# The norm of one MLP chunk split in two, its factors ahead of the head-row moves on GpSimd, its turn ahead of a denominators' broadcast

## The chip, the cores and the metric

One core of a Trainium2 chip. The metric is the device time of one execution in microseconds (us). The kernel before takes 203.77 us (median of 6 executions, 203.6 to 209.71). Each execution is fast or slow; a slow one is over 1.5% above the fastest of its kernel.

Each kernel was executed five or six times beside the kernel before, and **one** execution left the trace that the profile shows. For the kernel before it is one more execution (204.51 us), which is not among the six.

## The reference, cut to what matters

```python
xn = layernorm(x)                        # x: 2048 x 512, bf16
s  = attention(xn) @ wo                  # 32 heads of 16, window of 8, dilation 2
h  = gelu(layernorm(xn) @ w1)            # then parts of h shifted by rows
x1 = xn + shifted(h) @ w2
g  = silu(x1 + gelu(layernorm(x1) @ w3) @ w4)     # w3: 512 x 1376
return x + s * g
```

The kernel works on rows of even and odd position ("parity" 0 and 1) and on four chunks of 512 rows. While TensorE does the attention of parity 0, unit by unit ("turns" 0 to 7), it also makes x1 of the chunks. Each x1 chunk is normalised on VectorE, stored to DRAM, and loaded back transposed ("turned"), because w3's matmuls need it with the features on the partitions. After the last unit come w3's matmuls, chunk after chunk.

## The kernel before: the parts that matter

```python
def layer_stats(src, name, lo, hi):      # VectorE: bn_stats, bn_aggr for each 128-row tile
    ...
    rsqrt_eps(rstd, mv[:, :, 1])         # two small GpSimd instructions: "the factors"

def ln3_norm(c, a=0, b=TPC):             # VectorE: (x - mean) * rstd for tiles a..b
    ...
    if b < TPC:
        return
    ln3_store(c)                         # SyncE: 512 KB to x1n_dram (L514)

def ln3_turn(c):                         # SyncE: transposing load into x1nT[c] (L519)
    nc.sync.dma_start_transpose(out=x1nT[c], in_=x1n_dram[c * CH : (c + 1) * CH, :])

def spread(p, lo, hi, q, ws, es):        # head-row moves: 8 DMAs for one w (L261)
    ...
def normalise_dn(p, r):   ...            # SyncE: reload denominators (L678)
def normalise_mid(p, r):  ...            # VectorE reciprocal (L697), SyncE store (L698)
def normalise_rr(p, r):   ...            # SyncE: broadcast load, 368 KB for (0, 0) (L707)
def normalise_end(p, r):  ...            # VectorE multiply (L714)

# late[n]: what is issued at the end of attention turn n
late[6] += [lambda: ln3_norm(1), lambda: normalise_dn(0, 1), lambda: ln3_turn(1)]
...
for n, p, r in ((3, 0, 0), (6, 0, 1), (N1 + 3, 1, 0), (N1 + 6, 1, 1)):
    ...
    if (p, r) != (0, 1):
        late[n + 2].append(lambda p=p, r=r: normalise_mid(p, r))
        late[n + 2].append(lambda p=p, r=r: normalise_rr(p, r))
for w in range(2):
    late[3 + 2 * w].append(lambda w=w: spread(1, 0, CUT, nc.gpsimd, (w,)))
```

SyncE issues its DMAs in program order, and one that waits holds up those behind it: in the trace of before it issued nothing from 79.99 to 83.28 us, while a broadcast waited. "Landing" below is the moment when a DMA's completion shows in the trace; "granted clock" is the share of TensorE's full clock that the throttle granted.

The softmax here doesn't subtract the row's maximum and nothing guards it: scores larger than these inputs give would overflow.

Of the kernel before, what the change touches and what calls it, by code (L numbers as in the profile page):

```python
# [15 lines left out]
def kernel(  # L16
# [14 lines left out]
    nc = tc.nc  # L31
# [52 lines left out]
    def at(kb, n, m):  # L84
        ar, o = (arenas[0], int(kb * KB)) if kb < 170 else (arenas[1], int((kb - 176) * KB))
        return ar[:, o : o + int(n * m)].rearrange("p (n m) -> p n m", n=n)
# [44 lines left out]
    for c in range(NCH):  # L131
        p, k = c // 2, c % 2
# [123 lines left out]
    def spread(p, lo, hi, q=nc.sync, ws=(0, 1), es=(0, 1)):  # L256
        for w in ws:
            for e in es:
                for gr in range(4):
                    r = 32 * gr + DH * e  # L260
                    q.dma_start(  # L261
                        out=(kT, qT)[w][e][r : r + DH, :, lo:hi], in_=kq[p][w][r : r + DH, :, lo:hi]
                    )
# [236 lines left out]
    def ln3_norm(c, a=0, b=TPC):  # L500
        p, k = c // 2, c % 2
        x_c = xn[p][:, k * TPC : (k + 1) * TPC, :]
        for lo, hi, mv, rstd in l3[c]:
            for j in range(max(lo, a), min(hi, b)):
                nc.vector.tensor_scalar(
                    out=xn3[:, j, :], in0=x_c[:, j, :], scalar1=mv[:, j - lo, 0:1],
                    scalar2=rstd[:, j - lo : j - lo + 1], op0=ALU.subtract, op1=ALU.mult,
                )
        if b < TPC:
            return  # L510
        ln3_store(c)

    def ln3_store(c):
        nc.sync.dma_start(  # L514
            out=x1n_dram[c * CH : (c + 1) * CH, :].rearrange("(i q) d -> q i d", q=P), in_=xn3
        )

    def ln3_turn(c):
        nc.sync.dma_start_transpose(out=x1nT[c], in_=x1n_dram[c * CH : (c + 1) * CH, :])  # L519
# [155 lines left out]
    def normalise_dn(p, r):  # L675
        n = H * runs[p][r][3] // P
        dn = small.tile([P, n], BF16, name="dn", tag="dn")
        nc.sync.dma_start(out=dn, in_=rrs[p, r][0].rearrange("h (a m) -> (h a) m", a=P // 8))  # L678
        rrs[p, r][0] = dn

    def pack(p, r):
        _, _, ra, rw = runs[p][r]
        for jj in range(2):
            for cg in range(4):
                hh = 4 * jj + cg
                nc.gpsimd.dma_start(  # L686
                    out=oT[p][DH * hh : DH * (hh + 1), :, ra : ra + rw],
                    in_=orw[p, r][32 * cg : 32 * cg + DH, jj],
                )

    def normalise_mid(p, r):
        _, _, ra, rw = runs[p][r]
        n = H * rw // P
        dn, rden_d = rrs[p, r]
        rb = small.tile([P, n], BF16, name="rb", tag="rb")
        with nc.allow_low_precision("bf16 weights"):
            nc.vector.reciprocal(out=rb, in_=dn)  # L697
        nc.sync.dma_start(out=rden_d.rearrange("h (a m) -> (h a) m", a=P // 8), in_=rb)  # L698

    def normalise_rr(p, r):  # L700
        _, _, ra, rw = runs[p][r]
        dn, rden_d = rrs[p, r]
        if p == 0 and r:
            rr = orws[r % 2][:, 0 : ND * rw]
        else:
            rr = at(rr_at[r % 2] if p else B0 + 8, 1, ND * rw)[:, 0, :]
        nc.sync.dma_start(out=rr, in_=rden_d.unsqueeze(1).to_broadcast([8, DH, ND * rw]))  # L707
        rrs[p, r] = rr
# [157 lines left out]
    late = {n: [] for n in range(len(order) + 4)}  # L866

    def st3(n, *ts):
        for t in ts:
            late[n].append(lambda t=t: ln3_stats(t // 4, t % 4, t % 4 + 1))  # L870
# [4 lines left out]
    st3(3, 4)  # L875
    st3(4, 5, 6)
    st3(5, 7)
    late[6] += [lambda: ln3_norm(1), lambda: normalise_dn(0, 1), lambda: ln3_turn(1)]

    w4s = [w4_tile(t) for t in range(S // P)]  # L880
    fill = {0: (0, 1), 1: (2,), 3: (3,), 4: (4,), 5: (5,), 7: (6,), 8: (7,)}
# [22 lines left out]
    for n, p, r in ((3, 0, 0), (6, 0, 1), (N1 + 3, 1, 0), (N1 + 6, 1, 1)):  # L904
        if (p, r) != (0, 1):
            late[n].append(lambda p=p, r=r: pack(p, r))
        if p:
            late[n].append(lambda p=p, r=r: normalise_dn(p, r))
        if (p, r) != (0, 1):
            late[n + 2].append(lambda p=p, r=r: normalise_mid(p, r))  # L910
            late[n + 2].append(lambda p=p, r=r: normalise_rr(p, r))
    late[N1 + 7].append(lambda: normalise_end(1, 0))
    CUT = 480
    for w in range(2):
        late[3 + 2 * w].append(lambda w=w: spread(1, 0, CUT, nc.gpsimd, (w,)))

    prev = None

# [73 lines left out]
    for t in range(8, 15):  # L992
# [5 lines left out]
        p, i = fq.pop(0)  # L998
# [50 lines left out]
```

## Time and profile before

| | before |
|---|---|
| median, six executions | 203.77 us |
| profiled execution | 204.51 us (span of the trace 202.7) |
| TensorE busy | 193.9 us, 96% of the span |
| wait of TensorE for chunk 1's turned rows | 0.75 us |

The span runs from the first to the last instruction; the measured time is about 1.8 us longer. The two ordinary fast executions that I had when I predicted took 203.62 and 203.76. (Of the six in the table four took 203.6 to 203.8, one 204.65, and one, 209.71, is slow.)

### The profile page before, as it was taken

How to read it: one execution, taken by the hardware profiler on the slowest of the kernel's cores; microseconds unless marked ns; L12 is line 12 of the kernel's file. 1: busy time of each engine (PE TensorE's matmuls, PEld its weight loads, DVE VectorE, ACT ScalarE, POOL GpSimd, SP SyncE). 2: the span in 40 equal slices, each digit the busy share in tenths (PEclk: the TensorE clock that was granted, in tenths of full speed). 3: DMA queues.
4: the chain of work that ended last, by engine and by line, in shares of the span. 5: the costliest groups of instructions: out<-in, count | busy, mean ns of one | idle time of the engine just before them, and what ended most of it. 6: DMA issues, size and time to landing. Idle time of an engine off the chain costs nothing.

```text
span 202.7 us, 4886 instructions
## 1 busy us (share of the span) xinstructions
PE 193.9 (96%) x1939; PEld 95.2 (47%) x1967; DVE 134.2 (66%) x263; ACT 131.5 (65%) x155; POOL 73.8 (36%) x146
## 2 busy tenths in 40 slices
PE   7899999999999999999899999999999999999991
PEld 2585445444444444444444444444455444444460
DVE  5788889735298988888610501188567968676683
ACT  2367665859988888885555575998788879212120
POOL 4899516200033195978750000003830590700000
PEclk9999999999999999999999999999999999999998
DMA  5993266367750189487979846793130052554221
GB/s 133 359 349 96 83 145 120 62 102 115 151 205 5 52 178 137 80 236 157 185 220 198 258 102 102 156 333 126 32 55 5 8 126 35 115 168 155 86 78 53
DMA packets 33734, 27.17 MB, mean 134 GB/s; under 512 B 14720, under 2 KB 31624, under 8 KB 33712
## 3 DMA queue, kind: packets, MB, share of 16 engines
q1 hardware_dynamic: 31520, 23.64, 46.7%
q0 software_dynamic: 2048, 3.09, 8.4%
q8 instruction: 15, 0.25, 0.5%
q10 hardware_dynamic: 144, 0.13, 0.2%
q14 instruction: 7, 0.06, 0.1%
HBM read 12.82 MB, written 4.98 MB: 88 GB/s over the span
## 4 chain that ended last, share of the span: by engine, by line
PE 83%; DMA 7%; DVE 3%; POOL 3%; issue 2%; DVEq 0%; POOLq 0%
PE w_ps L567 18%; PE w_ps L530 13%; PE qk_ps L432 8%; PE v_ps L596 7%; PE w_ps L488 7%; PE w_ps L465 7%; PE wo_ps L742 6%; PE s_ps L621 6%; PE o_ps L644 4%; PE qk_ps L450 4%; DMA x1n_dram<-arena 3%; DMA arena<-x1n_dram 3%; PE w_ps L547 1%; DMA arena<-in_A_x_dram 1%; DVE l0s L311 1%
## 5 line engine op out<-in xcount | busy, mean ns | idle before, releaser
L626 ACT ACTIVATE arena<-s_ps 128x960 bf16<-128x960 f32 (+1 forms) x68 | 62.8, 976 | 12.3 <-PE s_ps L621 12.3
L567 PE MATMUL w_ps<-arena 128*128 128x512 bf16 (+1 forms) x164 | 39.3, 368 | 0.5 <-issue 0.2
L534 ACT ACTIVATE arena<-w_ps 128x1024 bf16<-128x1024 f32 x20 | 20.5, 1025 | 14.2 <-PE w_ps L530 14.2
L686 POOL DMA_DIRECT2D arena<-orw x48 | 24.9, 526 | 5.8 <-DVE orw L656 5.8
L567 PEld LDWEIGHTS <-arena 128*128 128x128 bf16 x187 | 17.6, 98 | 18.9
L530 PEld LDWEIGHTS <-arena 128*128 128x128 bf16 x160 | 15.4, 98 | 20.2 <-DMA arena<-x1n_dram 1.2
L752 POOL TENSOR_TENSOR arena<-arena 128x512 bf16<-128x512 bf16 x6 | 7.7, 1302 | 47.1 <-DVE arena L751 47.1
L432 PE MATMUL qk_ps<-arena 128*128 128x512 bf16 (+1 forms) x109 | 20.2, 332 | 0.6 <-ACT arena L328 0.5
L656 DVE CAST orw<-o_ps 128x960 bf16<-128x960 f32 (+1 forms) x17 | 19.7, 1157 | 1.5 <-PE o_ps L644 1.4
L573 DVE TENSOR_TENSOR arena<-w_ps,arena 128x512 bf16<-128x512 f32 (+1 forms) x17 | 11.2, 659 | 14.2 <-PE w_ps L567 14.1
L601 DVE CAST v_aug<-v_ps 128x512 bf16<-128x512 f32 x17 | 11.7, 690 | 10.3 <-PE v_ps L596 10.2
L582 ACT ACTIVATE arena<-arena 128x512 bf16<-128x512 bf16 (+1 forms) x9 | 5.3, 584 | 20.4 <-DVE arena L573 20.4
L530 PE MATMUL w_ps<-arena,arena 128*128 128x512 bf16 x78 | 17.3, 379 | 0.9 <-DMA arena<-x1n_dram 0.7
L530 PE MATMUL w_ps<-arena 128*128 128x512 bf16 x78 | 17.7, 379 | 0.2
L596 PE MATMUL v_ps<-wv_sb,arena 128*128 128x512 bf16 x68 | 17.5, 380 | 0.0
L621 PEld LDWEIGHTS <-arena 32*128 32x128 bf16 x544 | 10.2, 92 | 14.5 <-issue 14.4
L621 PE MATMUL s_ps<-arena 32*128 32x120 bf16 (+1 forms) x544 | 15.9, 213 | 0.0
L488 PE MATMUL w_ps<-arena 128*128 128x512 bf16 x64 | 15.3, 380 | 0.0
L492 DVE TENSOR_TENSOR arena<-w_ps,arena 128x512 bf16<-128x512 f32 x16 | 10.4, 684 | 7.2 <-PE w_ps L488 7.2
L439 ACT CAST arena<-qk_ps 128x1024 bf16<-128x1024 f32 x11 | 11.1, 1021 | 6.0 <-PE qk_ps L432 6.0
L432 PEld LDWEIGHTS <-arena 128*128 128x128 bf16 x112 | 10.8, 98 | 8.3 <-issue 0.5
L280 POOL TENSOR_SCALAR l3r<-l3m 128x1 f32<-128x1 f32 (+2 forms) x11 | 2.6, 236 | 33.2 <-DVE l3m L289 33.1
(108 smaller groups left out, 275.9 us busy)
## 6 DMA issues: line engine op xcount, KB each, us to landing
x1n_dram<-arena SPq DMA_DIRECT2D x5, 512.0 KB, 4.0
arena<-in_A_x_dram SPq DMA_DIRECT2D x4, 512.0 KB, 6.0
arena<-in_A_x_dram SPq DMA_DIRECT2D x6, 256.0 KB, 6.8
out_dram<-arena SPq DMA_DIRECT2D x6, 256.0 KB, 2.1
arena<-in_B_w_dram SPq DMA_DIRECT2D x1, 1376.0 KB, 7.0
arena<-in_B_w_dram SPq DMA_DIRECT2D x1, 1280.0 KB
arena<-arena SPq DMA_DIRECT2D x16, 72.0 KB, 2.5
arena<-arena SPq DMA_DIRECT2D x16, 68.0 KB, 2.6
```

What stands on the lines that cost most here:

```text
L432: nc.tensor.matmul(pt[:, b, hh * w : (hh + 1) * w], lhsT=wqk_sb[:, dt, nt * P : (nt + 1) * P], rhs=xnT[p][:, dt, k * CH + hh * w : k * CH ...
L465: nc.tensor.matmul(pt[:, b, :], lhsT=w1_sb[:, dt, g * P : (g + 1) * P], rhs=xn2T[c][:, dt, :], start=(dt == 0), stop=(dt == ND - 1),)
L488: nc.tensor.matmul(pt, lhsT=w2_src(p, g, m0), rhs=w2_sb[:, g, :], start=(g == 0), stop=(g == ND - 1))
L530: nc.tensor.matmul(pt[:, ft % 2, :], lhsT=w3_sb[:, dt, ft * P : (ft + 1) * P], rhs=x1nT[c][:, dt, :], start=(dt == 0), stop=(dt == ND - 1),)
L534: nc.scalar.activation(h3(c, 2 * a, 2), pt, AF.Gelu_apprx_tanh)
L567: nc.tensor.matmul(pt, lhsT=h3(c, ft, 1)[:, 0, jj * P : (jj + 1) * P], rhs=w, start=(ft == 0), stop=(ft == NF - 1),)
L596: nc.tensor.matmul(vp[:nk, :], lhsT=xnT[p][:, dt, k0 : k0 + nk], rhs=wv_sb[:, dt, :], start=(dt == 0), stop=(dt == ND - 1),)
L621: nc.tensor.matmul(st[:nk, b, i * nq : (i + 1) * nq], lhsT=kT[e][r : r + 32, dt, k0 : k0 + nk], rhs=qT[e][r : r + 32, dt, q0 : q0 + nq], s ...
L626: nc.scalar.activation(prv[:nk, 2 * h : 2 * h + 2], st[:nk, :, 0 : 4 * nq], AF.Exp, scale=SCALE)
L656: nc.vector.tensor_copy(out=orw[p, r][:, :, :, q0 - ra : q0 - ra + nq], in_=op[:, :, 0 : 4 * nq].rearrange("p j (s q) -> p j s q", q=nq),)
L686: nc.gpsimd.dma_start(out=oT[p][DH * hh : DH * (hh + 1), :, ra : ra + rw], in_=orw[p, r][32 * cg : 32 * cg + DH, jj],)
L742: nc.tensor.matmul(pt, lhsT=oT[p][:, dt, i * P : (i + 1) * P], rhs=wo_sb[:, dt, ds], start=(dt == 0), stop=(dt == ND - 1),)
```

## The change

The intent: turn chunk 1 earlier, so that TensorE does not wait for it when chunk 0's w3 is done.

```diff
-    late[6] += [lambda: ln3_norm(1), lambda: normalise_dn(0, 1), lambda: ln3_turn(1)]
+    late[5].append(lambda: ln3_norm(1, 0, 2))
+    late[6] += [
+        lambda: ln3_norm(1, 2, 4), lambda: normalise_mid(0, 0), lambda: normalise_dn(0, 1),
+        lambda: ln3_turn(1), lambda: normalise_rr(0, 0),
+    ]
@@ in the loop over (n, p, r)
-        if (p, r) != (0, 1):
+        if p:
             late[n + 2].append(lambda p=p, r=r: normalise_mid(p, r))
             late[n + 2].append(lambda p=p, r=r: normalise_rr(p, r))
@@
-        late[3 + 2 * w].append(lambda w=w: spread(1, 0, CUT, nc.gpsimd, (w,)))
+        late[5].append(lambda w=w: spread(1, 0, CUT, nc.gpsimd, (w,)))
```

It has two halves: the **GpSimd and VectorE half** (all 16 moves in turn 5 behind the factors; the norm two tiles at a time) and the **SyncE half** (the denominators' reciprocal and its store behind the norm, the broadcast behind the turn).

## The prediction

> **What bounds the kernel now.** I read the page first, its busy times:
>
> ```profile
> PE 193.9 (96%) x1939; PEld 95.2 (47%) x1967; DVE 134.2 (66%) x263; ACT 131.5 (65%) x155; POOL 73.8 (36%) x146
> ```
>
> TensorE is busy for 193.9 of 202.7 us and the granted clock is 0.996, so no change to norms and moves can gain more than TensorE's idle time. Next I read the table of busy time by 10 us stretches: TensorE has 9.6 to 9.95 us of every 10 from 10 to 190 us, with one exception, which is where this change acts:
>
> ```profile
> 90.00:100.00 10.00, 9.25 (x44) 4.05 (x43) 7.75 (x19) 5.49 (x6) 6.75 (x14) 1.00 0.75 169
> ```
>
> The timeline of TensorE around it shows one hole (the bracket is the idle time ahead of the row and what ended it):
>
> ```profile
> 89.09 7.08 PE L530 MATMUL w_ps<-arena 128*128 128x512 bf16 x31
> 96.92 1.25 PE L530 MATMUL w_ps<-arena,arena 128*128 128x512 bf16 x5 [0.75 <-DMA arena<-x1n_dram]
> ```
>
> The first row ends at 96.17: w3 of chunk 0 is finished. The second starts at 96.92: w3 of chunk 1 waited 0.75 us for its transposed rows, x1nT[1]. The chain that ended last, in order of time, tells how that data came:
>
> ```profile
> 82.48 0.57 POOL l3r L281
> 83.05 0.22 POOL l3r L280
> 83.34 0.64 POOL l3r L281
> ...
> 84.89 0.42 DVE arena L505
> 85.32 0.02 issue
> 85.33 6.21 DMA x1n_dram<-arena
> 91.55 0.02 issue
> 91.56 5.31 DMA arena<-x1n_dram
> ```
>
> GpSimd makes the factors of tiles 5, 6 and 7 one after the other; VectorE normalises the last tile at 84.89; the store takes 6.21 us and the turn (the transposing load) 5.31. These 11.5 us are most of the page's "DMA 7%" of the chain, but that share is not what can be won: everything before 96.17 is hidden behind TensorE. **The ceiling of this change is 0.75 us, 0.37% of 203.76.**
>
> Two timelines tell why the chain is late. GpSimd:
>
> ```profile
> 75.43 1.52 POOL L261 DMA_DIRECT2D arena<-arena  x3
> 78.04 0.51 POOL L261 DMA_DIRECT2D arena<-arena  x1 [1.09 <-PE s_ps L621]
> 79.05 1.08 POOL L261 DMA_DIRECT2D arena<-arena  x2 [0.49 <-DMA arena<-orw]
> 81.00 1.13 POOL L261 DMA_DIRECT2D arena<-arena  x2 [0.87 <-DMA arena<-orw]
> 82.15 0.25 POOL L280 TENSOR_SCALAR l3r<-l3m 128x1 f32<-128x1 f32 x1
> ```
>
> Eight head-row moves, with their waits, hold GpSimd from 75.43 to 82.13, while VectorE's statistics of tiles 5 and 6 are done at 74.74 and of tile 7 at 79.00 (its timeline). And SyncE's queue:
>
> ```profile
> 79.64 0.35 SPq L698 DMA_DIRECT2D rden_d<-rb  x1
> 83.28 0.69 SPq L707 DMA_DIRECT2D arena<-rden_d  x1
> 84.03 0.53 SPq L669 DMA_DIRECT2D den_d<-orw  x1
> 85.33 0.39 SPq L514 DMA_DIRECT2D x1n_dram<-arena  x1
> ```
>
> The broadcast of parity 0's first denominators (L707, 368 KB) stands waiting until 83.28 for its own store, holds the next denominators back, and is queued just ahead of the norm's store (L514).
>
> **What the Trainium skill says.** "DMA: Bandwidth & Descriptors", section "Anatomy of one DMA — SWDGE (gpsimd) path", gives a fixed cost of about 2.0 us plus bytes at 436 GB/s, mostly the write receipt, and says that waits for semaphores are made on the issuing sequencer before dispatch. The trace agrees with the second: SyncE issued nothing from 79.99 to 83.28. For the first, the norm's store is 524288 bytes: an estimate of 2.0 + 1.2 = 3.2 us from that page, whereas the four stores of this trace take 3.9 to 6.2, median 4.2; I use the trace. "Perfetto Trace Analysis", section "Summary: the profiler window per engine type", says that a DMA instruction's slice leaves out the movement of the data; the trace agrees (slice 0.39 us, landing 6.21), so I read landings. "SBUF — State Buffer", section "Who interferes with whom", says that VectorE in a two-port mode blocks GpSimd's descriptor writing. I see no such cost: GpSimd's moves have a median of 514 ns and a maximum of 591 beside a busy VectorE.
>
> **The change part by part.** No arithmetic and no transfer is added or removed; all of it is order.
>
> 1. The first eight moves go from turn 3 to turn 5, behind the factors. GpSimd is free at 75.43 after its packing. Tiles 5 and 6 cost 0.25 + 0.57 us each and are done by 77.1; tile 7 follows its statistics at 79.00 and is done at 79.85. Before, that was 84.86: 5.0 us earlier. The 16 moves then stand together from 79.9; 16 x 0.53 = 8.5 us puts their end at 88.4, or about 89.5 with some waits. Before it was 89.29. So chunk 2's factors, begun at 89.31, should hardly move, and the moves themselves are not read before parity 1's first scores at 125.8.
>
> 2. The norm in two parts: tiles 4 and 5 at VectorE's turn 5 (79.0, in the 0.70 us that the reciprocal at 78.92 leaves), tiles 6 and 7 in turn 6, at 83.15 where the four stand now. Two take about 0.7 us: the store can go at 83.85 in place of 85.33, **1.5 us earlier**.
>
> 3. The order on SyncE. The denominators' broadcast goes behind the turn, and its reciprocal behind the norm (83.9 to 84.6). The store is no longer queued behind 368 KB of broadcast, though it now shares with the tail of the 16 moves (60 KB each). Between the median of 4.2 us and the 6.2 of now I choose 5.3: landing at 89.2. The turn then takes its 5.31 us: 94.5. TensorE wants it at 96.17. So **the data comes about 2.4 us earlier, 0.75 of which shows in the time and 1.6 is slack.** Sum: 203.76 - 0.75 = 203.0.
>
> **The rivals.**
>
> A. *The wait moves to chunk 2's turn.* Before, that turn is issued at 98.26 and TensorE starts chunk 2 at about 105.56, without a wait. By the other turns (5.3 to 7.5 us) it landed between 103.6 and 105.8, so its slack is 0 to 2 us, and TensorE will now ask 0.75 earlier, at 104.8. Against: chunk 2's norm ends at 93.96 by VectorE's and GpSimd's own pace, and SyncE, done with chunk 1's turn earlier, can issue its store at 94.0 in place of 94.33. For: the broadcast (368 KB), now issued near 91.5, runs beside that store. If it costs 1 us, 0.2 to 0.8 us of the gain is lost.
>
> B. *The late denominators hold VectorE.* The multiply L714 runs at 93.87 now. The broadcast, issued behind the turn at about 91.3 and needing about 4.7 to 5.5 us (the last one of the trace was issued at 116.86 and its reader began at 121.83), lands at 96.5 to 97, so VectorE waits some 3 us there, and behind it stand chunk 3's statistics and norm. Chunk 3's store goes from 101.47 to about 104.5, its turn from 105.78 to about 108.4, landing at 113.7 to 115.9. TensorE's packed w3 reads it first in its third group: 114.36 - 0.75 + 1.8 = 115.4. So mostly hidden, at worst 0.5 us lost. The w4 load behind it, issued at 109.4 now, would go at 112.4 and is read at 126.2: hidden.
>
> C. *The moves, now in one block, hold GpSimd past chunk 2's factors* (needed at 92 to 93). It takes over 3 us more of waits than I count to show. Unlikely.
>
> D. *The store gains nothing*, because the 16 moves (960 KB in some 9 us) slow it to 7 us or more: landing at 90.9, the turn at 96.2, and still almost all of the 0.75 is won.
>
> **Range and chances.** 0.75 is won in full with about one chance in two (203.0); A and B each take a part of it with perhaps one in four to three, on average 0.5 of loss. That gives 203.2. The low end is the full gain and 0.5 of scatter (two of the three runs of before lie within 0.14, the third, 209.71, looks like a slower state): 202.5. The high end is a loss of all of the gain and 0.3 more: 204.0. 2% is 4.1 us, five times the ceiling: faster by over 2% can't come from this hole, and slower needs a wait that I don't see or a slow state in the runs. So within 2%: 0.97.
>
> **What the profile after should show.** TensorE's hole at 96 is gone or under 0.2 us. The factors' row of tile 7 ends near 80; the norm's store is issued near 83.9 and the turn before 90.5. All 16 moves are in one block from 80 to about 89. VectorE has a new wait ahead of L714, on the broadcast, of 2 to 4 us (B's first half). Any new TensorE wait stands ahead of chunk 2's (near 105) or chunk 3's w3 (near 115). I am wrong if TensorE's total idle time does not fall by 0.4 to 0.8 us, or if a hole opens past 125, where parity 1's scores, w4 and the output projection read what SyncE's later queue brings.

## The result, and the profile after

The changed kernel takes **203.43 us** (median of 6, 203.35 to 203.52), the kernel before 203.77. The ratio of the fast executions is 0.9979 (95% interval 0.9961 to 0.9997). Ratios here are the mean of one kernel's fast executions over the mean of the other's in the same rounds, so not quite the ratio of the medians.

Busy time of the engines, from the page of the changed kernel:

```profile
PE 194.3 (96%) x1967; PEld 94.8 (47%) x1967; DVE 133.8 (66%) x263; ACT 131.4 (65%) x155; POOL 73.3 (36%) x146
```

TensorE is as busy as before, within 0.4 us, in a span that is 1.0 us shorter (201.7). Its timeline where the hole was:

```profile
89.23 7.08 PE L530 MATMUL w_ps<-arena 128*128 128x512 bf16 x32
96.15 2.11 PE L530 MATMUL w_ps<-arena,arena 128*128 128x512 bf16 x9
```

Chunk 1's w3 starts at 96.15 and the second row has no bracket: the hole is gone. SyncE's queue of the changed kernel (start, length of the issue, line):

```profile
82.21 0.58 SPq L669 DMA_DIRECT2D den_d<-orw  x1
84.10 0.40 SPq L514 DMA_DIRECT2D x1n_dram<-arena  x1
84.74 0.34 SPq L698 DMA_DIRECT2D rden_d<-rb  x1
85.18 0.94 SPq L678 DMA_DIRECT2D dn<-den_d  x1
89.90 2.08 SPq L519 DMA_TRANSPOSE arena<-x1n_dram  x1
92.06 0.68 SPq L707 DMA_DIRECT2D arena<-rden_d  x1
```

The store (L514) goes at 84.10, the turn (L519) at 89.90 in place of 91.56, the broadcast (L707) last. GpSimd:

```profile
79.63 0.58 POOL L281 TENSOR_TENSOR l3r<-l3r,nhalf 128x1 f32<-128x1 f32 x1
80.25 7.99 POOL L261 DMA_DIRECT2D arena<-arena  x14
88.82 1.08 POOL L261 DMA_DIRECT2D arena<-arena  x2 [0.58 <-DMA rden_d<-rb]
89.92 0.25 POOL L280 TENSOR_SCALAR l3r<-l3m 128x2 f32<-128x2 f32 x1
```

The last factor of the chunk is done at 80.2, the 16 moves stand behind it as one block, and chunk 2's factors start at 89.92 (89.31 before). VectorE has the new wait that was foreseen, for the late broadcast:

```profile
97.99 0.93 DVE L714 TENSOR_TENSOR arena<-arena,arena 128x1472 bf16<-128x1472 bf16 x1 [3.88 <-DMA arena<-rden_d]
```

In the chain that ended last, DMA had 7% of the span before and has 1% now (E1, an execution of the kernel before without the wait, has 1% too, so this share follows the wait). All this is as planned. But the trace of before held 0.75 us to win, and the medians differ by 0.34 us. The experiments are about that gap.

### The profile page after: what moved, and what is told of

The parts are those of the page before. It is cut to its first block, busy times and chain, and to the rows that moved or that the text cites. A ratio compares the mean times of both kernels' runs of the same rounds, so it can differ in the third digit from the quotient of the medians.

```text
span 201.7 us, 4915 instructions
## 1 busy us (share of the span) xinstructions
PE 194.3 (96%) x1967; PEld 94.8 (47%) x1967; DVE 133.8 (66%) x263; ACT 131.4 (65%) x155; POOL 73.3 (36%) x146
## 4 chain that ended last, share of the span: by engine, by line
PE 91%; DVE 3%; POOL 2%; DMA 1%; issue 1%; ACT 0%; DVEq 0%
PE w_ps L567 19%; PE w_ps L530 17%; PE qk_ps L432 9%; PE v_ps L596 8%; PE w_ps L488 7%; PE w_ps L465 7%; PE s_ps L621 7%; PE wo_ps L742 7%; PE o_ps L644 5%; PE qk_ps L450 4%; PE w_ps L547 1%; DMA arena<-in_A_x_dram 1%; DVE l0s L311 1%; POOL l0r L315 1%; PE tr_ps L384 1%; DVE arena L747 1%
## 5 line engine op out<-in xcount | busy, mean ns | idle before, releaser
L567 PE MATMUL w_ps<-arena 128*128 128x512 bf16 (+1 forms) x173 | 40.1, 368 | 0.0
L567 PEld LDWEIGHTS <-arena 128*128 128x128 bf16 x187 | 17.6, 98 | 18.9
L530 PEld LDWEIGHTS <-arena 128*128 128x128 bf16 x160 | 15.5, 98 | 19.2 <-issue 0.8
L752 POOL TENSOR_TENSOR arena<-arena 128x512 bf16<-128x512 bf16 x6 | 7.2, 1225 | 43.3 <-DVE arena L586 32.3
L530 PE MATMUL w_ps<-arena 128*128 128x512 bf16 x80 | 17.8, 379 | 0.1
L488 PE MATMUL w_ps<-arena 128*128 128x512 bf16 x64 | 15.3, 380 | 0.0
L465 PE MATMUL w_ps<-arena 128*128 128x512 bf16 x64 | 14.8, 379 | 0.0
```

Of the source, the lines that this page charges most:

```text
L465: nc.tensor.matmul(pt[:, b, :], lhsT=w1_sb[:, dt, g * P : (g + 1) * P], rhs=xn2T[c][:, dt, :], start=(dt == 0), stop=(dt == ND - 1),)
L488: nc.tensor.matmul(pt, lhsT=w2_src(p, g, m0), rhs=w2_sb[:, g, :], start=(g == 0), stop=(g == ND - 1))
L530: nc.tensor.matmul(pt[:, ft % 2, :], lhsT=w3_sb[:, dt, ft * P : (ft + 1) * P], rhs=x1nT[c][:, dt, :], start=(dt == 0), stop=(dt == ND - 1),)
L567: nc.tensor.matmul(pt, lhsT=h3(c, ft, 1)[:, 0, jj * P : (jj + 1) * P], rhs=w, start=(ft == 0), stop=(ft == NF - 1),)
```

## The experiments

All ran with five rounds beside the kernel before. Those of one group shared a chip and the executions of before: E1 to E4, E5 to E8, E9 to E12. The medians of before in the three groups were 203.69, 203.65 and 203.65 us.

### E1: the kernel before once more

No edit.

> The kernel before once more, as noise floor and as a second draw of its profile. Its profiled run took 204.51 us where its unprofiled fast ones took 203.6 to 203.8. Theory (the hole is the same in every execution): ratio 1.000 within 0.001 and a hole of 0.6 to 0.9 us again ahead of chunk 1's w3 near 96. Rival (the profile showed a longer hole than most executions have): ratio 1.000, hole of 0 to 0.5 us, span 201.9 to 202.2.

Median 203.63 us, ratio 0.9992 (0.9965 to 1.0019). TensorE's timeline, the same program as before:

```profile
89.17 7.08 PE L530 MATMUL w_ps<-arena 128*128 128x512 bf16 x31
96.09 2.11 PE L530 MATMUL w_ps<-arena,arena 128*128 128x512 bf16 x9
```

**There is no hole.** The turn was issued at 91.44 and the data came just in time: its last landing mark in the packed trace lies at 95.98 us. This profiled execution took 203.66 us and spans 201.9 us; the one of the first profile took 204.51 and spans 202.7. The rival is right: the first profile had caught an execution with a hole, and, going by their times, most have none.

### E2: the GpSimd and VectorE half alone

```diff
+    late[5].append(lambda: ln3_norm(1, 0, 2))
+    late[6] += [lambda: ln3_norm(1, 2, 4), lambda: normalise_dn(0, 1), lambda: ln3_turn(1)]
     # normalise_mid(0, 0), normalise_rr(0, 0) stay in turn 5; both spreads in turn 5
```

> Only the GpSimd and VectorE half: moves behind the factors, norm in two parts; the denominators' reciprocal and broadcast stay ahead on SyncE. Theory (the half needs the other): the broadcast still waits for its own store, now issued near 80.5, so SyncE is blocked until about 84 and the norm's store goes at about 85.4 as before, queued behind 368 KB: landing after 91, hole as before, ratio to before 1.000. Rival (late factors were the cause): store near 83.9, hole gone, ratio as the whole change, 0.998.

Median 203.77 us, ratio 0.9998 (0.9969 to 1.0027): nothing gained. My reason was partly wrong, as SyncE's queue shows:

```profile
80.27 0.36 SPq L698 DMA_DIRECT2D rden_d<-rb  x1
81.89 0.70 SPq L707 DMA_DIRECT2D arena<-rden_d  x1
82.64 0.54 SPq L669 DMA_DIRECT2D den_d<-orw  x1
83.92 0.39 SPq L514 DMA_DIRECT2D x1n_dram<-arena  x1
87.85 0.33 SPq L678 DMA_DIRECT2D dn<-den_d  x1
90.72 2.17 SPq L519 DMA_TRANSPOSE arena<-x1n_dram  x1
```

The broadcast was not held up: its own store landed in 1.6 us here, against 3.6 before. So the store of the norm left at 83.92, 1.3 us earlier than in E1. Behind the broadcast, though, it took 6.8 us, and the turn went at 90.72, only 0.7 earlier than E1's 91.44. (A difference of 0.7 us between two traces is within the scatter: the turn of before's order went between 90.03 and 91.74 us in the traces of before, E1, E4, E5, E11 and E12.) The profiled execution has no hole, and one of the six took 204.42 us.

### E3: the SyncE half alone

```diff
-    late[6] += [lambda: ln3_norm(1), lambda: normalise_dn(0, 1), lambda: ln3_turn(1)]
+    late[6] += [
+        lambda: ln3_norm(1), lambda: normalise_mid(0, 0), lambda: normalise_dn(0, 1),
+        lambda: ln3_turn(1), lambda: normalise_rr(0, 0),
+    ]
-        if (p, r) != (0, 1):
+        if p:
```

> Only the SyncE half: reciprocal behind the norm, broadcast behind the turn; moves and norm as before. Theory: the store still goes at about 85.3 for want of factors, but with no broadcast ahead it lands in about 4.5 us, at 89.8; the turn ends near 95.1, under the 96.17 that TensorE needs: hole gone, ratio 0.998, like the whole change. Rival (both halves are needed): hole of 0.3 us or more remains, ratio over 0.999.

Median 203.32 us (203.25 to 203.7), ratio 0.9973 (0.9948 to 0.9998): all of the gain (why, the section on the tail tells). The store left at 85.16 and the turn at 90.13. So the store landed in 5.0 us at most, against 6.2 in E1 and before, with the broadcast no longer ahead of it. The other traces narrow this: from store to turn it is 5.0 and 4.8 us in E3 and its repeat E10, and 5.1 to 6.5 in the six traces with the broadcast ahead and the moves as before, E12 and E4 being the shortest (5.1 and 5.2). So the broadcast ahead of the store costs something, but how much differs from execution to execution.

E3's traced execution is its longest, 203.70 us (the others took 203.25 to 203.48), and it has a wait that I first overlooked, ahead of **chunk 2**:

```profile
96.05 17.67 PE L530 MATMUL w_ps<-arena,arena 128*128 128x512 bf16 x78
```

In E1 the same row takes 17.43 us. In the chain that ended last, chunk 2's store takes 6.57 us from 94.04, its turn lands at 104.88, and TensorE goes on at 104.92: rival A of the prediction, worth 0.24 us.

### E4: nothing to wait for (wrong result)

```diff
-                    ..., rhs=x1nT[c][:, dt, :],
+                    ..., rhs=x1nT[0 if c == 1 else c][:, dt, :],     # in w3_pair
```

> Wrong result on purpose: in the kernel before, chunk 1's w3 pairs read chunk 0's transposed rows, so that TensorE has nothing to wait for at 96; all transfers stay. It measures the ceiling in ordinary executions. Theory (hole 0.75 us in all executions): ratio 0.9963. Rival (most executions have a hole of about 0.35 us): ratio 0.998, the same as the whole change's 0.9979.

Median 203.63 us (203.48 to 203.71), ratio 0.9984 (0.9959 to 1.0008). Neither guess fits: the ceiling that I had read as 0.75 us is worth 0.06 us in the median. None of the six executions is above 204 us, where three of before's eleven fast ones in these rounds are. **So the hole that the change closes is hardly where its 0.34 us in the median come from.**

### Where the steady part is: the tail

I compared the traces from their ends. From the start of chunk 0's w3 to the start of the last output projection takes 109.66 us in E1, E4 and the changed kernel alike. What differs is VectorE's last four instructions. E1 (the kernel before):

```profile
197.19 0.42 DVE L747 SCALAR_TENSOR_TENSOR arena<-wo_ps,arena 128x256 bf16<-128x256 f32 x1
197.65 0.29 DVE L752 TENSOR_TENSOR arena<-arena 128x256 bf16<-128x256 bf16 x1
198.08 0.42 DVE L747 SCALAR_TENSOR_TENSOR arena<-wo_ps,arena 128x256 bf16<-128x256 f32 x1
198.54 0.29 DVE L752 TENSOR_TENSOR arena<-arena 128x256 bf16<-128x256 bf16 x1
```

The changed kernel:

```profile
197.25 0.42 DVE L747 SCALAR_TENSOR_TENSOR arena<-wo_ps,arena 128x256 bf16<-128x256 f32 x1
197.71 0.29 DVE L752 TENSOR_TENSOR arena<-arena 128x256 bf16<-128x256 bf16 x1
197.91 0.42 DVE L747 SCALAR_TENSOR_TENSOR arena<-wo_ps,arena 128x256 bf16<-128x256 f32 x1
198.37 0.29 DVE L752 TENSOR_TENSOR arena<-arena 128x256 bf16<-128x256 bf16 x1
```

The last multiply (the second L747) follows the add ahead of it by 0.43 us in one, by 0.20 in the other. The add lasts 0.29, so in the kernel before VectorE stands still for some 0.14 us; E4's timeline puts 0.16 us there down to "issue", that is, to no wait that the profile shows. E2 and E4, with before's time, have 0.43 and 0.45; E3, whose median has the whole gain, has 0.21. Nothing in the change touches these instructions. But when I counted all of VectorE's records in the traces, its semaphore waits included, the slow ones had 325 and the fast ones 326: the new order makes VectorE wait once more on a semaphore, and every later instruction stands one place further on. In what follows "the tail" is the time from the last multiply's own wait, which begins 0.01 us after the add, to the multiply: 0.42 or 0.19 us. E5 and E6 test this.

### E5: before plus one idle instruction; E6: the change minus one

```diff
 # E5, in the kernel before, on VectorE while it is idle at the start
     nc.vector.memset(nhalf[:], -0.5)
+    nc.vector.memset(nhalf[:], -0.5)
 # E6, in the changed kernel: two memsets of one tile become one
+        if p == 0:
+            nc.vector.memset(hT[p][:, :, 0 : M + 2 : M + 1], 0.0)
+            continue
         nc.vector.memset(hT[p][:, :, 0:1], 0.0)
         nc.vector.memset(hT[p][:, :, M + 1 : M + 2], 0.0)
```

> The kernel before with one memset more on VectorE in its idle head (one constant written twice). The whole change and the SyncE half have 326 VectorE records in their traces, before and the other kernels 325, and in the two with 326 VectorE's last multiply follows its wait for TensorE by 0.19 us in place of 0.42. Theory T (the steady part of the gain is this tail, decided by how many instructions stand ahead in VectorE's stream): tail 0.19, the lowest of its runs down by 0.2 us, ratio 0.9990, while a run in four or so near 204.5 stays. Rival (the steady gain comes from the order of the transfers): tail 0.42, lowest run as before.

> The changed kernel with one VectorE instruction fewer (two memsets of one tile in one), back to 325 records. Theory T: tail back to 0.42, lowest run near 203.55 instead of 203.35, no run near 204.5; ratio to before 0.9985. Rival: as the changed kernel, 203.4 median and tail 0.19.

| | records | tail, us | lowest | median | ratio to before |
|---|---|---|---|---|---|
| before, same rounds | 325 (E1) | 0.42 (E1) | 203.52 | 203.65 | |
| E5: before plus one | 326 | 0.19 | 203.28 | 203.46 | 0.9983 (0.9962 to 1.0003) |
| E6: change minus one | 325 | 0.42 | 203.55 | 203.63 | 0.9995 (0.9977 to 1.0013) |

A useless memset gives the kernel before the changed kernel's tail and low end; taking an instruction out takes both away from the changed kernel. Each ratio alone is not clear of noise; all executions together are. Of the 63 of programs with 325 records (before, E1, E2, E4, E6) 61 took 203.52 us or more; of the 38 with 326 or 327 (the change, E3, E5, E9 to E12) 34 took 203.52 or less (E7 and E8, with their copy, left aside). This is also why E2, with 325 records, gains nothing in the median and E3, with 326, everything. The end of E6's tail, to be read like the two above:

```profile
197.71 0.29 DVE L755 TENSOR_TENSOR arena<-arena 128x256 bf16<-128x256 bf16 x1
198.14 0.42 DVE L750 SCALAR_TENSOR_TENSOR arena<-wo_ps,arena 128x256 bf16<-128x256 f32 x1
```

E5's profile also caught a second execution with the hole, 203.97 us long while its others took 203.28 to 203.50:

```profile
96.62 1.69 PE L531 MATMUL w_ps<-arena,arena 128*128 128x512 bf16 x7 [0.52 <-DMA arena<-x1n_dram]
```

### E7 and E8: the same useless copy, before and after

```diff
 def ln3_store(c):
+    if c == 1:
+        extra = dram.tile([CH, D], BF16, name="extra_d")
+        nc.sync.dma_start(out=extra, in_=A_x.flatten_outer_dims()[0:CH, :])    # 512 KB
```

> The kernel before with one useless 512 KB copy on SyncE's queue just ahead of chunk 1's norm store. Theory (before has no slack: TensorE's need and the data's arrival coincide): everything it adds shows, about 2 us: a hole ahead of chunk 1's w3 of 1.5 to 2.5 us in every run, median 205.1 to 206.1. Rival (before has slack, and the hole of the first profile was something else): under 0.5 us more.

> The same useless copy in the changed kernel. Theory (the change bought about 1.5 us of slack that ordinary executions don't need): 0.3 to 1.0 us of hole, median 203.7 to 204.4, about 1.5 us under the same copy in the kernel before. Rival (no slack bought): as far above the changed kernel as the other is above before.

**Before** goes to 208.52 us (207.4 to 210.66, the last one counted as slow), ratio 1.0231 (1.0191 to 1.0272): 4.9 us more, twice what I expected. **The changed kernel** stays at 203.37 us in the median (203.24 to 205.9): five of its six executions hide the copy entirely. So before had too little slack for the copy, and the change did buy slack. The landings in the packed traces say the same. TensorE needs chunk 1's rows at about 96.1 us; the turn's last landing mark lies between 94.5 and 96.9 in the six traces with before's moves, norm and order on SyncE (before, E1, E4, E5, E11, E12), and between 93.8 and 95.1 in those of the SyncE half (the change, E3, E6, E9, E10). So before's slack is 1.5 us in one execution and missing in another. (E7 happens to have 326 records and the short tail of 0.20 us, so beside before it looks 0.2 us too good.) TensorE in E7's profiled execution:

```profile
98.68 19.13 PE L533 MATMUL w_ps<-arena,arena 128*128 128x512 bf16 x78 [2.43 <-DMA arena<-x1n_dram]
```

The hole is 2.43 us, and the 78 recorded w3 matmuls behind it take 19.13 us against 17.43 in E1, because the granted clock falls: it is 0.90, 0.50 and 0.74 in the three stretches of 2 us from 98 to 104, which makes 1.7 us of lost clock. In this execution the wait cost its own time and 1.7 us more.

E8's profiled execution is its longest, 205.9 us (still counted as fast), and shows where the slack ends:

```profile
96.34 8.81 PE L533 MATMUL w_ps<-arena,arena 128*128 128x512 bf16 x39 [0.22 <-DMA arena<-x1n_dram]
107.25 1.04 PE L533 MATMUL w_ps<-arena,arena 128*128 128x512 bf16 x4 [2.10 <-DMA arena<-x1n_dram]
```

Chunk 1's hole is 0.22 us; the large one, 2.10 us, stands ahead of **chunk 2**. When something is late, the delay now comes out one chunk further on, as it did without any copy in E3. Chunk 2's turn goes at 99.1 to 100.6 us in the five traces of the SyncE half without the copy, against 97.9 to 98.5 in the six of before's order. That the late broadcast, now issued 2 to 3 us ahead of chunk 2's store, slows this store (4.9 to 6.6 us to the turn, against 3.8 to 4.4) fits all of them; no run isolates it. After this hole of 2.10 us the granted clock stayed at 1.00.

### E9 to E12: the sum, and two left-over questions

E9 is the changed kernel and E10 the SyncE half, both again, without an edit. E11 is E4 with E5's memset. E12 is the kernel before with two extra memsets:

```diff
 # E12; E11 has one of the two, and E4's edit
     nc.vector.memset(nhalf[:], -0.5)
+    nc.vector.memset(nhalf[:], -0.5)
+    nc.vector.memset(nhalf[:], -0.5)
```

> The changed kernel once more, beside the SyncE half on one chip. Theory: 203.35 to 203.5, no run over 204, ratio to before 0.998.

> The SyncE half once more (before, 203.32). Theory (the GpSimd and VectorE half buys only slack that goes unused): the same as the changed kernel within 0.1 us. Rival (that half costs something): 0.1 us or more below the changed kernel again.

> Wrong result on purpose: the kernel before with chunk 1's w3 reading chunk 0's rows, so no wait there, and with one VectorE memset more. Theory (the change's gain is these two things and no more): all runs 203.25 to 203.5, as the changed kernel. Rival (something of the order itself also pays): 203.55 or more, or runs near 204.5.

> The kernel before with two memsets more on VectorE (327 records). If every other position pays, the tail is 0.42 again and the lowest run 203.5; if the boundary is of a longer period, the tail stays 0.19 and the lowest run 203.3. I lean to the longer period, 60 to 40.

| | median (lowest to highest) | ratio to before | tail, us |
|---|---|---|---|
| E9: the change | 203.47 (203.26 to 203.49) | 0.9988 (0.9976 to 1.0000) | 0.19 |
| E10: SyncE half | 203.32 (203.28 to 203.42) | 0.9984 (0.9971 to 0.9997) | 0.20 |
| E11: no need, plus one | 203.32 (203.28 to 203.45) | 0.9985 (0.9973 to 0.9997) | 0.20 |
| E12: before plus two | 203.43 (203.27 to 205.17) | 1.0004 (0.9979 to 1.0030) | 0.20 |

E11 closes the sum for the median: the old order, with the wait and the tail taken away by other means, is as fast as the change. For the executions above 204 us this group says little, as before itself had none among its ten fast ones in these rounds. E12 shows that it isn't every second place that pays. In all my traces the last multiply is slow as record 319 of VectorE's stream (counted from 0) and fast as 320 or 321. E10 is 0.15 us below E9, as my rival had it; the executions of the two overlap and I found no difference in the traces that explains it, so whether the GpSimd half costs 0.1 us stays open.

## Why the prediction was right or wrong

The time, 203.43 us, lies in the range, 0.23 above the number; the change is within 2%, as said. That it lies so near is luck: I expected a gain of 0.56 us from the hole, and of the 0.34 measured (0.18 in E9) 0.2 come from a place that I had not looked at. By its steps:

**Part 1, the factors: right in the trace, but not needed.** The last factor is done at 80.2 (predicted 79.85), the moves end at 89.9 (88.4 to 89.5). E2, this half with its norm in two, gains nothing in time; E3, without it, gains everything.

**Part 2, the store 1.5 us earlier: near.** It went at 84.10 where 83.85 was predicted and 85.33 was before.

**Part 3, the order on SyncE: right, and the part that matters for the transfers.** I chose a landing of 5.3 us; the turn went 5.8 us after the store, and E3's went 5.0 after. The rows' last landing mark is at 94.45 us, 2.4 us ahead of the 96.87 of before's trace, as I said, but only 1.5 ahead of E1's 95.98. E7 and E8 confirm the slack. One reading was wrong: "the four stores" that take 3.9 to 6.2 us are three. `prof` pairs no landing with chunk 0's store, and its turn followed 3.0 us later.

**Rivals.** B's first half came as described, VectorE waiting 3.88 us for the broadcast (2 to 4 said), and stayed hidden. A did not show in the changed kernel's trace, though chunk 2's turn went at 99.50 in place of 98.26; it cost 0.24 us in E3's trace and 2.10 in E8's. C, a block of moves that delays chunk 2's factors, came to 0.6 us and cost nothing. D did not come: the store's 5.8 us are nearer to the 5.3 that I chose than to D's 7.

**My sign of being wrong can't be read.** I asked that TensorE's total idle time fall by 0.4 to 0.8 us. By the pages it is 8.8 us in before's trace, 9.2 in E1's, which has no hole, and 7.4 in the changed kernel's; 28 matmul records are missing from the first two and not from the third, so these differences say nothing.

**The step that failed is the sum's only term: "0.75 of which shows in the time".** I took the hole of one profiled execution for a property of all. I had the warning in hand: the two ordinary fast executions of before were 0.75 and 0.89 us faster than the profiled one, by just about the hole. What stood in its place are two smaller things.

1. *In the median, the tail.* One more record in VectorE's stream moves its last multiply from place 319 to 320 and takes 0.22 us off the end. E5 and E6 show it in both directions. No step of the prediction had it.

2. *In the mean, the rare executions.* Among the fast executions of all programs that keep before's order on SyncE and its need for chunk 1's rows (before, E1, E2, E5, E12), 9 of 60 took 204.39 to 205.17 us. Among those with the SyncE half or without the need (the change, E3, E4, E6, E9, E10, E11), none of 38 did; the highest is 203.75. That these 9 are executions with the hole is inferred: they left no trace. But the two traced executions with a hole (0.75 and 0.52 us) are 0.85 us above E1's traced one and 0.51 above E5's median, from the start of chunk 0's w3 to that of the last output projection they take 110.59 and 110.35 us against E1's 109.66, and without the need none occur. Three more executions of before, 207.93 to 209.71 us, were left out as slow. The two whose clock is on record have 0.987 and 0.989, much like E7's six (207.4 to 210.66 us, 0.982 to 0.996); whether they are longer holes, no trace shows.

What the change does is therefore: an accident at the end that gives 0.2 us, in every trace of it, and slack in the middle that, as far as the times tell, spares about one execution in seven 0.7 to 1.5 us. It pays for the slack of chunk 1 with some of chunk 2's.

What stays open: why place 319 is slow, why the store's landing scatters so between executions of one program, and the 0.15 us between E9 and E10.

## What to carry to other kernels

Before sizing a gain from a hole in a profile, compare the profiled execution's time with the ordinary ones: where it is longer by about the hole, as here, most executions may not have it, and removing it may narrow the spread more than it moves the median. Take the need away, with a wrong result, to measure a ceiling. For gains of a tenth of a per cent, make a control that only shifts instructions by one place; otherwise an accident is put down to the idea.

## What the Trainium skill lacked or had wrong

- *No page that I found has it; "Runtime: NRT & Kernel Launch", section "Instruction fetch mechanics", comes nearest,* saying that instructions are refilled in blocks of 256 and that crossing a block's end is mostly hidden. Here VectorE's last multiply starts 0.42 to 0.44 us after its wait as record 319 of the stream, 0.19 to 0.20 us as record 320 or 321, in all 14 traces (slow in five of them). Whether fetching is the cause no run shows.
- *"TensorE: Matmul & The Clock Gate", section "What's actually happening",* says that the array falls to half clock after at least one idle window of about 3.4 us. In E7 a hole of 2.43 us was followed by a granted clock of 0.50 (100 to 102 us) and 1.7 us of slower matmuls; in E8 a hole of 2.10 us left it at 1.00. The effect is as described; the idle time that it took here is shorter.
- *"DMA: Bandwidth & Descriptors", section "Anatomy of one DMA — SWDGE (gpsimd) path":* its fit, given for the other path, makes 3.2 us for the 512 KB store on SyncE's queue, an estimate. Chunk 0's store, which starts at 69.38 us in before's trace, where the DMA share is 0.00 from 69 to 70, was followed by its turn after 3.0 us, so the estimate is about right there. Chunk 1's took 4.8 to 6.8 us in the traces without the copy. The size is the same, so what else moved at the time must have made the difference; that fit has no term for it.
- How many matmul records a profile leaves out, no page that I read says: here 1939 are in the trace of before and 1967 in that of the change, of the same program on TensorE. The small pauses that this makes in TensorE's rows, put down to "issue", are no time lost: E1, with 1939, takes the same 109.66 us from chunk 0's w3 to the last output projection as the change.
